# Converting the first MLP's float64 weights a feature at a time on VectorE and ScalarE, and squaring its first blocks from SBUF

## The chip, the cores and the metric

The kernel runs on one core of one Trainium2 chip. The metric is the device time of one execution in microseconds (us); the times below are medians of several executions.

## What is computed

Three stages follow one another on 3072 tokens of width 512:

```python
state = gamma * state + k[t] (outer) v[t]; y[t] = scale * q[t] @ state    # retention, 4 x 8 heads, 768 steps
x = y as (3072, 512)
r = maximum(x @ w_in, 0); x = (s * (r * r) + b) @ w_out                   # first MLP, d_ff = 2048
logits = x @ w_gate; tokens are assigned greedily to 8 experts, 384 each
out = maximum(x @ w1[e], 0) @ w2[e]                                       # second MLP, by expert
```

`w_in` and `w_out` arrive as float64. The device reads them as pairs of 32-bit words and makes two fp32r tiles of each: a high part `h` and a low part `l`. Products are formed from three matmuls (high by high, high by low, low by high).

## The kernel before, in words

The tokens are cut into 12 blocks of 256, each of two chunks of 128. The first MLP's 2048 hidden features are cut into `NF` = 16 groups, called features here; feature f has 128 rows of `w_in` (half n = 2f) and 128 of `w_out` (half n = 2f + 1), each half a tile of 128x512 numbers, or 512 KB of float64.

**Order of work.** The program writes out the order of every engine's instructions itself (`manual_schedule`). `Weave` holds a planned time `t`. Each unit of PE work (`wv.unit(cost, fn)`) adds its cost; before it is issued, every side generator whose due time has come is stepped, and each `yield` adds its number of nanoseconds to that due time. So the numbers in `CY` set how densely conversion steps lie between PE's units. They set an order, not a time: each engine then runs its own list, waiting where data or a buffer is missing.

**Prologue.** `load_chunk` (line 175) asks SP for the q, k, v and decay tiles of chunks 0 to 5, with the raw weights of halves 0 to 5 between them (lines 572 to 579, `conv_load`, line 228). The loop at line 588 alternates between `attn3`, which computes retention for blocks 0 to 2, and the weight conversion, whose steps are stretched there by `PRO` = 1.5; it stops converting early once `PN` = 2 is in `READY`. GpSimd (POOL) scales q and v (lines 201 and 204).

**Conversion** (`conv_gen`, line 233), for each half n, 512 numbers to a partition. ScalarE (ACT) squares the upper words (line 239). VectorE (DVE) shifts and masks the upper words (line 262), puts sign and exponent back (line 266), sets tiny numbers to zero by means of the squares (line 269), takes the exponent alone (line 275) and multiplies the lower word by it (line 279). ACT rounds to `h` (line 249), POOL subtracts `h` (line 251) and adds the low word (line 253) to give `l`. The raw words are read at a stride of two words, and all results go into packed tiles.

**First MLP, blocks 0 to 2** (`moe1`, line 544, called at line 597). For each feature and each of three blocks, `h_unit` (line 416) issues 12 matmuls (line 425) into one of two PSUM banks and ACT takes the Relu into `r` (line 428); `r_split` (line 433) squares it on ACT into `rh` (line 436), squares it again on DVE from the PSUM bank (line 440), and POOL forms `rl`, the low part (line 441). Two units later `x_unit` (line 450) issues 6 matmuls (line 458). That makes 48 pairs of an `h_unit` and an `x_unit`, planned at 1320 and 1300 ns. `hu` (line 552) first makes sure that the weights it needs have been converted. `r` has two buffers, `rh` and `rl` three.

**Later blocks** go one at a time, with retention and the gate's dot products (line 481) beside them. There `r_split` is called without the PSUM bank: the squares wait in `LOW`, and `low_parts` (line 444) squares `r` from SBUF (line 447) and subtracts `rh` (line 448), both on DVE, at the next `hu`. Blocks 3 to 11, the gate, the assignment and the second MLP follow.

Of the kernel before, what the change touches and what calls it, by code (L numbers as in the profile page):

```python
# [20 lines left out]
F32 = mybir.dt.float32  # L21
F32R = mybir.dt.float32r
BF = mybir.dt.bfloat16
F16 = mybir.dt.float16
I32 = mybir.dt.int32
U32 = mybir.dt.uint32
I64 = mybir.dt.int64
AF = mybir.ActivationFunctionType
OP = mybir.AluOpType
# [3 lines left out]
FAR = 1.0e6  # L33


TINY_WORD = 1.125 * 2.0 ** -15


class Side:
# [42 lines left out]
def kernel(  # L82
# [16 lines left out]
    stages=2,  # L99
    PRO=1.5,  # L100
    PN=2,
    CY=(560, 890),
    SY=(5500, 5200, 4200, 3000, 2600, 1200),
    IY=(1500, 2700, 900),
    LG=(900, 880),
# [13 lines left out]
    NF = w64.shape[0]  # L119
# [4 lines left out]
    TB = 256  # L124
# [6 lines left out]
    stage = ctx.enter_context(tc.tile_pool(name="stage", bufs=2))  # L131
# [4 lines left out]
    PE, ACT, DVE, POOL, SP = nc.tensor, nc.scalar, nc.vector, nc.gpsimd, nc.sync  # L136
# [17 lines left out]
    loads = p0.enter_context(tc.tile_pool(name="loads", bufs=2, side="right"))  # L154
# [3 lines left out]
    work = p1.enter_context(tc.tile_pool(name="work", bufs=2))  # L158
    xpool = p1.enter_context(tc.tile_pool(name="xpool", bufs=2))
    tmp = p1.enter_context(tc.tile_pool(name="tmp", bufs=6))  # L160
# [5 lines left out]
    def load_dec(j):  # L166

        if j < CPB:
            n = 2 * NF - 1 - 2 * CPB - j // 2
            QD[j] = wpool.tile([128, 512], F32, name=f"qdec{j}", tag=("h", "l")[j % 2] + str(n))  # L170
        else:
            QD[j] = loads.tile([128, 512], F32, name="qdec", tag="qdec")
        SP.dma_start(QD[j], dec[:, j % CPB * n0:(j % CPB + 1) * n0])

    def load_chunk(j):
        if j < CPB:

            ts = []
            for i in range(4):
                n = 2 * NF - 1 - 2 * j - i // 2  # L180
                tag = ("h", "l")[i % 2] + str(n)
                ts.append(wpool.tile([128, 512], F32, name=f"first{j}_{i}", tag=tag))
            for i in (0, 1, 3, 2):
                SP.dma_start(ts[i], qkv[j, :, i])
                if j == 0 and i in first:
                    first[i]()
            if j:
                load_dec(j)
        else:
            ts = []  # L190
            load_dec(j)
            for i in (0, 2):
                t = loads.tile([128, 2, 512], F32, name=f"q{i}", tag=f"q{i}")
                SP.dma_start(t, qkv[j, :, i:i + 2])
                ts += [t[:, 0, :], t[:, 1, :]]
        QKV[j] = ts

    def scale_chunk(j, q=POOL, v=POOL):
# [23 lines left out]

    W = {}
    RAW = {}
    NRAW = 6
    READY = set()

    def conv_load(n):
        pool, tag = ((stage, "sa"), (loads, "q0"), (loads, "q2"))[n // 2 % 3]
        RAW[n] = pool.tile([128, 512], I64, name="raw", tag=tag)  # L230
        SP.dma_start(RAW[n], w64[n // 2, n % 2])

    def conv_gen():
        sq = {}

        def square(n):
            hf = RAW[n].bitcast(F32).rearrange("p (n t) -> p t n", t=2)[:, 1, :]
            sq[n] = tmp.tile([128, 512], F32, name="tmp")
            ACT.activation(sq[n], hf, AF.Square)

        square(0)
        last = None

        def parts(step):
            n, a, p = last
            if step == 0:
                W[n] = (wpool.tile([128, 512], F32R, name=f"h{n}", tag=f"h{n}"),
                        wpool.tile([128, 512], F32R, name=f"l{n}", tag=f"l{n}"))
                ACT.activation(W[n][0], a, AF.Copy)
            elif step == 1:  # L250
                POOL.tensor_tensor(a, a, W[n][0].bitcast(F32), op=OP.subtract)
            else:
                POOL.tensor_tensor(W[n][1], a, p, op=OP.add)  # L253
                READY.add(n)

        for n in range(2 * NF):
            raw = RAW.pop(n)
            hi32 = raw.bitcast(I32).rearrange("p (n t) -> p t n", t=2)[:, 1, :]
            lo32 = raw.bitcast(U32).rearrange("p (n t) -> p t n", t=2)[:, 0, :]
            a = tmp.tile([128, 512], F32, name="tmp")  # L260
            ai = a.bitcast(I32)
            DVE.tensor_scalar(ai, hi32, 3, 0x3FFFFFFF, op0=OP.logical_shift_left, op1=OP.bitwise_and)  # L262
            if last:
                parts(0)
            yield CY[0]
            DVE.scalar_tensor_tensor(ai, hi32, -0x40000000, ai, op0=OP.bitwise_and, op1=OP.bitwise_or)  # L266
            yield CY[1]
            p = sq.pop(n)
            DVE.scalar_tensor_tensor(a, p, TINY_WORD * TINY_WORD, a, op0=OP.is_ge, op1=OP.mult)  # L269
            if last:  # L270
                parts(1)
            if n + 1 < 2 * NF:
                square(n + 1)
            yield CY[1]
            DVE.tensor_scalar(p.bitcast(I32), ai, -0x800000, None, op0=OP.bitwise_and)
            yield CY[0]
            if last:
                parts(2)
            DVE.scalar_tensor_tensor(p, lo32, 2.0 ** -52, p, op0=OP.mult, op1=OP.mult)
            if n + NRAW < 2 * NF:  # L280
                conv_load(n + NRAW)
            last = (n, a, p)
            yield CY[1]
        for step in range(3):
            parts(step)
            yield 600

    conv = Side(conv_gen())

# [126 lines left out]
    def h_unit(blk, f, hb):  # L416

        xh, xl = XT[blk]
        wh, wl = W[2 * f]
        ph = bank(hb)[:, 0:TB]  # L420
        n = 0
        for kc in range(KC):
            ks = slice(kc * 128, (kc + 1) * 128)
            for a, b in ((wh, xh), (wh, xl), (wl, xh)):
                PE.matmul(ph, a[:, ks], b[:, kc, :], start=(n == 0), stop=(n == 3 * KC - 1))  # L425
                n += 1
        r = work.tile([128, TB], F32, name="r", bufs=2)
        ACT.activation(r, ph, AF.Relu)  # L428
        return r, ph

    LOW = []

    def r_split(r, rh, rl, ph=None):


        ACT.activation(rh, r, AF.Square)  # L436
        if ph is None:
            LOW.append((r, rh, rl))
        else:
            DVE.scalar_tensor_tensor(r, ph, 0.0, r, op0=OP.max, op1=OP.mult)  # L440
            POOL.tensor_tensor(rl, r, rh.bitcast(F32), op=OP.subtract)
        return rh, rl

    def low_parts():
# [95 lines left out]
    def conv_until(n):  # L540
        while n not in READY:
            conv.step()

    def moe1(blks, xbs, lag, apart=0):


        units = []
        seq = [(f, i) for f in range(NF - apart) for i in range(len(blks))]
        seq += [(f, i) for i in range(len(blks)) for f in range(NF - apart, NF)]
        for n in range(len(seq) + lag):  # L550
            if n < len(seq):
                def hu(n=n):
                    f, i = seq[n]
                    conv_until(2 * f + 1)
                    low_parts()
                    r, ph = h_unit(blks[i], f, 2 + n % 2)
                    R2[blks[i], f] = r_split(r, work.tile([128, TB], F32R, name="rh", bufs=3),
                                             work.tile([128, TB], F32R, name="rl", bufs=3),
                                             ph if len(blks) > 1 else None)
                units.append((1320, hu))  # L560
            if n >= lag:
                def xu(n=n - lag):
                    f, i = seq[n]
                    if n + lag >= len(seq):
                        low_parts()
                    x_unit(blks[i], f, xbs[i])
                    if f == NF - 1:
                        x_out(blks[i])
                units.append((1300, xu))
        return units  # L570

    conv_load(0)
    load_chunk(1)
    conv_load(1)
    SP.dma_start(sb[:, 0:1], bass.AP(tensor=moe_s.tensor, offset=moe_s.offset, ap=[[0, 128], [1, 1]]))
    SP.dma_start(sb[:, 1:2], bass.AP(tensor=moe_b.tensor, offset=moe_b.offset, ap=[[0, 128], [1, 1]]))
    for j in range(2, CPB):
        load_chunk(j)
        conv_load(j)
    scale_chunk(0, DVE)  # L580

    def attn3():
# [5 lines left out]
    while not a3.done:  # L588
        if conv.due < a3.due and PN not in READY:
            t = conv.due  # L590
# [5 lines left out]
    wv = Weave([conv])  # L596
    for u in moe1((0, 1, 2), ((4, 5), (6, 7), (0, 1)), 2):
        wv.unit(*u)
    conv_until(2 * NF - 1)
    load_chunk(CPB)  # L600
    load_chunk(CPB + 1)
    scale_chunk(CPB)
# [59 lines left out]
    def h_pair(f):  # L662
        rs = []
        for i, blk in enumerate(pair):
            wv.unit(1320, lambda: rs.append(h_unit(blk, f, 2 + i)[0]))

        R4[f] = [wpool.tile([128, 512], F32R, name=f"{p}{2 * f}", tag=f"{p}{2 * f}") for p in "hl"]
        for i, r in enumerate(rs):
            r_split(r, *(t[:, i * TB:(i + 1) * TB] for t in R4[f]))
        low_parts()  # L670
# [415 lines left out]
    wv = Weave([Side(searches()), Side(indexes()), Side(weights())])  # L1086
# [91 lines left out]
```

## Time and profile before

| | us |
|---|---|
| median of 3 runs (1144.25 to 1148.87) | 1146.67 |
| the profiled execution | 1142.75 |
| its span, first to last instruction | 1141.0 |

| engine | busy us | share of the span |
|---|---|---|
| PE (TensorE matmul) | 1016.3 | 89% |
| DVE (VectorE) | 875.2 | 77% |
| ACT (ScalarE) | 385.1 | 34% |
| POOL (GpSimd) | 221.7 | 19% |

The durations used below come from the profiled execution, which is 3.9 us below the median of the runs. In a row of the trace `tmp<-raw x32` names the tile written, the tile read and the number of instructions; in a timeline the first number is the start from the beginning of the span and the second the duration. L425 is line 425. PE and PEld are TensorE's matmuls and weight loads. The first MLP's blocks 0 to 2 lie between 46.9 and 230 us of the span.

### The profile page before, as it was taken

To read this page: it belongs to the slowest core of one execution; us is meant where nothing else is said; L and a number is where in the kernel's file an instruction comes from. 1 tells how busy PE (TensorE), PEld (TensorE's weight loads), DVE (VectorE), ACT (ScalarE), POOL (GpSimd) and SP (SyncE) were. 2 spreads that over 40 slices of the span, in tenths; PEclk is the share of its full clock that TensorE was granted. 3 is DMA by queue.
4 is the path that set the end of the run, shared out by engine and by line. 5 is a ranking of instruction groups with operands and counts; after the bars stand their busy time and mean duration, and the time that the engine had idled before them with its cause. 6 is when DMAs were issued, how large, how long until landed. Compare 5 with 4: busy or idle time off the path is not lost.

```text
span 1141.0 us, 19761 instructions
## 1 busy us (share of the span) xinstructions
PE 1016.3 (89%) x7636; PEld 875.8 (77%) x7636; DVE 875.2 (77%) x2114; ACT 385.1 (34%) x802; POOL 221.7 (19%) x211
## 2 busy tenths in 40 slices
PE   5887877899999999999998999578789888888997
PEld 4766666788889898989897888467677677776786
DVE  3899999669999999999964744667787787867642
ACT  2433333332323323223333331223333443333442
POOL 3777777620000000000000000010111102011211
PEclk8999999999999999999999999869799999999999
DMA  9422222262212121221121000322333333343540
GB/s 323 144 90 92 93 93 82 96 193 75 66 47 75 56 57 56 57 74 58 35 95 32 2 1 11 138 66 85 120 102 121 111 108 134 95 133 116 166 139 28
DMA packets 35040, 104.51 MB, mean 92 GB/s; under 512 B 4737, under 2 KB 5249, under 8 KB 34945
## 3 DMA queue, kind: packets, MB, share of 16 engines
q1 hardware_dynamic: 30528, 89.60, 24.2%
q0 software_dynamic: 3840, 12.59, 3.3%
q8 instruction: 60, 0.98, 0.3%
q10 hardware_dynamic: 576, 1.05, 0.3%
q14 instruction: 36, 0.29, 0.1%
HBM read 90.64 MB, written 12.58 MB: 90 GB/s over the span
## 4 chain that ended last, share of the span: by engine, by line
PE 55%; DVE 23%; issue 11%; DMA 5%; ACT 2%; POOL 2%; SPq 0%; POOLq 0%; DVEq 0%; ACTq 0%
PE b L425 17%; PE b L458 13%; PE b L1012 6%; PE b L1033 5%; PE b L687 3%; DVE tmp L262 3%; DMA big<-x2d,idx 3%; DVE l L990 2%; PE b L794 2%; PE b L358 2%; PE b L368 2%; DVE tmp L266 2%; PE b L338 2%; DVE tmp L269 2%; DVE cmp L787 2%
## 5 line engine op out<-in xcount | busy, mean ns | idle before, releaser
L425 PE MATMUL b<-xh,h 128*128 128x256 f32 x704 | 201.7, 287 | 22.6 <-DVE r L440 20.9
L481 DVE SCALAR_TENSOR_TENSOR scr<-tmp,wg 128x512 bf16<-128x512 f32 x288 | 198.3, 689 | 6.8 <-ACT tmp L468 1.8
L425 PE MATMUL b<-xh,l 128*128 128x256 f32 x704 | 199.5, 283 | 0.9 <-POOL l L253 0.9
L425 PE MATMUL b<-xl,h 128*128 128x256 f32 x704 | 199.3, 283 | 0.0
L425 PEld LDWEIGHTS b<-xh,h 128*128 128x128 f32 x704 | 134.4, 191 | 39.2 <-DVE r L440 31.1
L428 ACT ACTIVATE r<-b 128x256 f32<-128x256 f32 x192 | 73.2, 382 | 253.3 <-PE b L425 225.5
L425 PEld LDWEIGHTS b<-xl,h 128*128 128x128 f32 x704 | 134.4, 191 | 4.8
L425 PEld LDWEIGHTS b<-xh,l 128*128 128x128 f32 x704 | 134.6, 191 | 1.5 <-POOL l L253 1.5
L458 PE MATMUL b<-h,rh 128*128 128x512 f32 x320 | 130.3, 407 | 0.0
L458 PE MATMUL b<-h,rl 128*128 128x512 f32 x320 | 127.1, 397 | 2.7 <-DVE rl L448 2.7
L458 PE MATMUL b<-l,rh 128*128 128x512 f32 x320 | 127.4, 398 | 0.0
L950 POOL DMA_INDIRECT big<-x2d,idx x24 | 26.1, 1088 | 355.1 <-issue 152.6
L1012 PE MATMUL b<-gh,h 128*128 128x384 f32 x256 | 93.1, 364 | 0.0
L1033 PE MATMUL b<-h,hh 128*128 128x512 f32 x192 | 81.0, 422 | 13.3 <-ACT hh L1015 13.3
L1012 PE MATMUL b<-gl,h 128*128 128x384 f32 x256 | 88.2, 344 | 1.7 <-DVE gl L962 1.7
L1012 PE MATMUL b<-gh,l 128*128 128x384 f32 x256 | 87.8, 343 | 0.0
L990 DVE TENSOR_TENSOR l<-eraw,h 128x512 fp32r<-128x512 f32 x128 | 82.3, 684 | 6.6 <-ACT h L989 6.6
L1033 PE MATMUL b<-h,hl 128*128 128x512 f32 x192 | 78.9, 411 | 8.0 <-DVE hl L1021 7.8
L447 DVE TENSOR_TENSOR r<-r 128x256 f32<-128x256 f32 x144 | 60.7, 421 | 25.6 <-ACT h L436 17.9
L1015 ACT ACTIVATE hh<-b 128x384 fp32r<-128x384 f32 x64 | 31.3, 489 | 138.3 <-PE b L1012 138.3
L1033 PE MATMUL b<-l,hh 128*128 128x512 f32 x192 | 76.9, 401 | 0.0
L458 PEld LDWEIGHTS b<-h,rl 128*128 128x128 f32 x320 | 61.0, 191 | 19.3 <-DVE rl L448 5.5
(193 smaller groups left out, 2054.2 us busy)
## 6 DMA issues: line engine op xcount, KB each, us to landing
eraw<-in_w_dram SPq DMA_DIRECT2D x64, 512.0 KB, 3.6
q<-in_qkv_dram SPq DMA_DIRECT2D x36, 512.0 KB, 4.7
raw<-in_w_dram SPq DMA_DIRECT2D x32, 512.0 KB, 3.5
first<-in_qkv_dram SPq DMA_DIRECT2D x24, 256.0 KB, 6.0
qdec<-in_dec_dram SPq DMA_DIRECT2D x24, 256.0 KB, 2.7
x2d<-tmp SPq DMA_DIRECT2D x20, 256.0 KB, 3.8
wg<-in_wgT_dram SPq DMA_DIRECT2D x4, 512.0 KB, 3.6
x2d<-tmp ACTq DMA_DIRECT2D x4, 256.0 KB, 2.0
```

The lines of the kernel that those rows point to most:

```text
L262: DVE.tensor_scalar(ai, hi32, 3, 0x3FFFFFFF, op0=OP.logical_shift_left, op1=OP.bitwise_and)
L425: PE.matmul(ph, a[:, ks], b[:, kc, :], start=(n == 0), stop=(n == 3 * KC - 1))
L428: ACT.activation(r, ph, AF.Relu)
L447: DVE.tensor_tensor(r, r, r, op=OP.mult)
L458: PE.matmul(X2[blk][t], a[:, ts], b, start=(f == 0 and i == 0), stop=(f == NF - 1 and i == 2))
L481: DVE.scalar_tensor_tensor(scr, x, 1.0, WG[e], op0=OP.mult, op1=OP.mult, accum_out=of[:, e:e + 1])
L687: PE.matmul(XB[c], a[:, cs], b, start=(f == 0 and i == 0), stop=(f == NF - 1 and i == 2))
L950: POOL.indirect_dma_start(out=xg[:, t, :], out_offset=None, in_=x2d[:, :], in_offset=bass.IndirectOffsetOnAxis(ap=IDX[i][:, t:t + 1], axis=0))
L990: DVE.tensor_tensor(lo, raw[:, a, :], hi.bitcast(F32), op=OP.subtract)
L1012: PE.matmul(PH[0], a[:, ks], b[:, kc, :], start=(kc == 0 and n == 0), stop=(kc == KC - 1 and n == 2))
L1015: ACT.activation(hh, PH[0], AF.Relu)
L1033: PE.matmul(Y[i, t], a[:, ts], b, start=(f == 0 and j == 0), stop=(f == NF2 - 1 and j == 2))
```

## The change

The conversion takes a whole feature at a time, 1024 numbers to a partition, and works in the raw tile itself: `hi` and `hf` are views of the upper words, `lo` and `lf` of the lower words, both at a stride of two words. ACT writes the magnitude of the upper words into a packed tile `c`. DVE takes its maximum with `ZERO_WORD`, shifts and masks it, puts sign and exponent back into the raw tile, takes the exponent alone into `c`, multiplies the lower words in the raw tile, and now also subtracts `h` and adds the low word, in halves. POOL has no part in it. The raw tile shares two buffers of 8 KB to a partition with the later chunks' q, k and v. `READY` counts features. `r_split` no longer has the form that reads the PSUM bank, so blocks 0 to 2 square from SBUF on DVE as the later ones do.

```diff
-TINY_WORD = 1.125 * 2.0 ** -15
+ZERO_WORD = 2.0 ** -15
...
-    CY=(560, 890),
+    CY=(700, 1200, 650),
...
+            t = loads.tile([128, 4, 512], F32, name="q")
             for i in (0, 2):
-                t = loads.tile([128, 2, 512], F32, name=f"q{i}", tag=f"q{i}")
-                SP.dma_start(t, qkv[j, :, i:i + 2])
-                ts += [t[:, 0, :], t[:, 1, :]]
+                SP.dma_start(t[:, i:i + 2], qkv[j, :, i:i + 2])
+                ts += [t[:, i, :], t[:, i + 1, :]]
...
-    NRAW = 6
...
-    def conv_load(n):
-        pool, tag = ((stage, "sa"), (loads, "q0"), (loads, "q2"))[n // 2 % 3]
-        RAW[n] = pool.tile([128, 512], I64, name="raw", tag=tag)
-        SP.dma_start(RAW[n], w64[n // 2, n % 2])
+    def conv_load(f):
+        RAW[f] = loads.tile([128, 1024], I64, name="raw", tag="q")
+        for i in range(2):
+            SP.dma_start(RAW[f][:, i * 512:(i + 1) * 512], w64[f, i])
...
     def conv_gen():
...
+        mag = {}
+
+        def magnitude(f):
+            mag[f] = stage.tile([128, 1024], F32, name="c", tag="sa")
+            ACT.activation(mag[f], RAW[f].bitcast(F32).rearrange("p (n t) -> p t n", t=2)[:, 1, :], AF.Abs)
+
+        magnitude(0)
+        for f in range(NF):
+            raw = RAW.pop(f)
+            (_, hi), (_, hf), (lo, _), (lf, _) = (
+                [v[:, t, :] for t in range(2)] for v in
+                (raw.bitcast(d).rearrange("p (n t) -> p t n", t=2) for d in (I32, F32, U32, F32)))
+            c = mag.pop(f)
+            ci = c.bitcast(I32)
+
+            DVE.tensor_scalar(c, c, ZERO_WORD, None, op0=OP.max)
+            yield CY[0]
+            DVE.tensor_scalar(ci, ci, 3, 0x3FFFFFFF, op0=OP.logical_shift_left, op1=OP.bitwise_and)
+            yield CY[0]
+
+            DVE.scalar_tensor_tensor(hi, hi, -0x40000000, ci, op0=OP.bitwise_and, op1=OP.bitwise_or)
+            for i in range(2):
+                n = 2 * f + i
                 W[n] = (wpool.tile([128, 512], F32R, name=f"h{n}", tag=f"h{n}"),
                         wpool.tile([128, 512], F32R, name=f"l{n}", tag=f"l{n}"))
-                ACT.activation(W[n][0], a, AF.Copy)
...
+                ACT.activation(W[n][0], hf[:, i * 512:(i + 1) * 512], AF.Copy)
+            yield CY[1]
+
+            DVE.tensor_scalar(ci, hi, -0x800000, None, op0=OP.bitwise_and)
             yield CY[0]
...
+            DVE.scalar_tensor_tensor(lf, lo, 2.0 ** -52, c, op0=OP.mult, op1=OP.mult)
             yield CY[1]
...
+            for i in range(2):
+                h, l = W[2 * f + i]
+                part = slice(i * 512, (i + 1) * 512)
+                DVE.tensor_tensor(hf[:, part], hf[:, part], h.bitcast(F32), op=OP.subtract)
+                yield CY[2]
+                DVE.tensor_tensor(l, hf[:, part], lf[:, part], op=OP.add)
+                if f + 1 < NF and not i:
+                    magnitude(f + 1)
+                yield CY[2]
+            if f + 2 < NF:
+                conv_load(f + 2)
+            READY.add(f)
...
-    def r_split(r, rh, rl, ph=None):
+    def r_split(r, rh, rl):
...
         ACT.activation(rh, r, AF.Square)
-        if ph is None:
-            LOW.append((r, rh, rl))
-        else:
-            DVE.scalar_tensor_tensor(r, ph, 0.0, r, op0=OP.max, op1=OP.mult)
-            POOL.tensor_tensor(rl, r, rh.bitcast(F32), op=OP.subtract)
+        LOW.append((r, rh, rl))
         return rh, rl
...
-                    conv_until(2 * f + 1)
+                    conv_until(f)
...
     conv_load(0)
     load_chunk(1)
-    conv_load(1)
...
     for j in range(2, CPB):
         load_chunk(j)
-        conv_load(j)
+        if j == 3:
+            conv_load(1)
...
-    conv_until(2 * NF - 1)
+    conv_until(NF - 1)
```

## Rows read from the trace of the kernel before

**Rows 1.** Windows: stretch, its us, then busy us and count of each engine, clock, DMA.
```profile
80.00:100.00 20.00, 15.04 (x89) 11.92 (x88) 19.66 (x23) 8.06 (x17) 15.08 (x13) 1.00 0.32 106
214.70:230.20 15.50, 15.50 (x93) 13.54 (x91) 2.43 (x6) 7.04 (x15) 9.60 (x11) 1.00 0.30 96
```

**Rows 2.** Waits of PE, 47 to 230 us: total, times, longest, in us.
```profile
PE b L425 <- DVE r L440: 32.1, 34, 2.1
```

**Rows 3.** Groups by line and shape, 0 to 225 us: busy us, mean ns.
```profile
L251 POOL TENSOR_TENSOR tmp<-tmp,h 128x512 f32<-128x512 f32 x32 | 51.7, 1617 | 3.0 <-ACT h L249 3.0
...
L279 DVE SCALAR_TENSOR_TENSOR tmp<-raw,tmp 128x512 f32<-128x512 uint32 x32 | 38.8, 1213 | 0.9
L269 DVE SCALAR_TENSOR_TENSOR tmp<-tmp 128x512 f32<-128x512 f32 x32 | 38.0, 1189 | 0.8
...
L262 DVE TENSOR_SCALAR tmp<-raw 128x512 int32<-128x512 int32 x32 | 36.4, 1136 | 0.0
L266 DVE SCALAR_TENSOR_TENSOR tmp<-raw,tmp 128x512 int32<-128x512 int32 x32 | 32.4, 1013 | 0.9
...
L275 DVE TENSOR_SCALAR tmp<-tmp 128x512 int32<-128x512 int32 x32 | 23.5, 735 | 0.7
...
L440 DVE SCALAR_TENSOR_TENSOR r<-b,r 128x256 f32<-128x256 f32 x47 | 19.4, 414 | 8.8 <-ACT rh L436 8.8
```

**Rows 4.** Timeline of POOL and of DVE, 42 to 45 us: start, duration.
```profile
44.99 1.52 POOL L251 TENSOR_TENSOR tmp<-tmp,h 128x512 f32<-128x512 f32 x1 [3.00 <-ACT h L249]
...
42.43 0.69 DVE L279 SCALAR_TENSOR_TENSOR tmp<-raw,tmp 128x512 f32<-128x512 uint32 x1
...
44.23 0.42 DVE L262 TENSOR_SCALAR tmp<-raw 128x512 int32<-128x512 int32 x1
44.69 0.69 DVE L266 SCALAR_TENSOR_TENSOR tmp<-raw,tmp 128x512 int32<-128x512 int32 x1
```

**Rows 5.** The page's group of L990; below it DVE's timeline, 251 to 258 us.
```profile
L990 DVE TENSOR_TENSOR l<-eraw,h 128x512 fp32r<-128x512 f32 x128 | 82.3, 684 | 6.6 <-ACT h L989 6.6
...
251.15 0.42 DVE L448 TENSOR_TENSOR rl<-r,rh 128x256 fp32r<-128x256 f32 x1
251.49 0.68 DVE L481 SCALAR_TENSOR_TENSOR scr<-tmp,wg 128x512 bf16<-128x512 f32 x1
...
256.51 0.42 DVE L447 TENSOR_TENSOR r<-r 128x256 f32<-128x256 f32 x1
...
257.38 0.69 DVE L481 SCALAR_TENSOR_TENSOR scr<-tmp,wg 128x512 bf16<-128x512 f32 x1
```

**Rows 6.** Groups of ACT by line and shape, 0 to 225 us.
```profile
L239 ACT ACTIVATE tmp<-raw 128x512 f32<-128x512 f32 x32 | 21.5, 676 | 60.6 <-POOL l L253 60.6
L249 ACT ACTIVATE h<-tmp 128x512 fp32r<-128x512 f32 x32 | 20.2, 632 | 36.0 <-DVE tmp L269 35.9
L436 ACT ACTIVATE rh<-r 128x256 fp32r<-128x256 f32 x47 | 19.6, 418 | 1.5
...
L428 ACT ACTIVATE r<-b 128x256 f32<-128x256 f32 x47 | 17.5, 372 | 10.0 <-PE b L425 9.9
```

**Rows 7.** Timeline of PE, the stage's first matmul and one pair near its end.
```profile
46.88 0.39 PE L425 MATMUL b<-xh,h 128*128 128x256 f32 x1 [1.41 <-DVE xls L377]
...
216.18 0.28 PE L425 MATMUL b<-xhs,h 128*128 128x256 f32 x1
...
217.62 0.40 PE L458 MATMUL b<-h,rh 128*128 128x512 f32 x1
...
219.00 0.28 PE L425 MATMUL b<-xh,h 128*128 128x256 f32 x1
...
229.96 0.39 PE L458 MATMUL b<-h,rl 128*128 128x512 f32 x1
```

**Rows 8.** Timeline of DVE, 214.6 us: the first square after the last conversion.
```profile
214.60 0.41 DVE L440 SCALAR_TENSOR_TENSOR r<-b,r 128x256 f32<-128x256 f32 x1
```

**Rows 9.** The window 10 to 20 us, and the page's row of raw's loads.
```profile
10.00:20.00 10.00, 4.85 (x64) 4.46 (x64) 1.88 (x3) 1.19 (x3) 3.80 (x4) 0.66 1.03 351
...
raw<-in_w_dram SPq DMA_DIRECT2D x32, 512.0 KB, 3.5
```

More of the change, by code (lines that the diff above doesn't have):

```diff
@@ L224 @@
     RAW = {}
-    NRAW = 6
     READY = set()
-    def conv_load(n):
-        pool, tag = ((stage, "sa"), (loads, "q0"), (loads, "q2"))[n // 2 % 3]
-        RAW[n] = pool.tile([128, 512], I64, name="raw", tag=tag)
-        SP.dma_start(RAW[n], w64[n // 2, n % 2])
+    def conv_load(f):
+        RAW[f] = loads.tile([128, 1024], I64, name="raw", tag="q")
+        for i in range(2):
+            SP.dma_start(RAW[f][:, i * 512:(i + 1) * 512], w64[f, i])
     def conv_gen():
[L234 to L246, printed above, removed]
+        mag = {}
[17 more added lines that the diff above has]
+                n = 2 * f + i
@@ L247, in parts @@
                 W[n] = (wpool.tile([128, 512], F32R, name=f"h{n}", tag=f"h{n}"),
                         wpool.tile([128, 512], F32R, name=f"l{n}", tag=f"l{n}"))
-                ACT.activation(W[n][0], a, AF.Copy)
-            elif step == 1:
-                POOL.tensor_tensor(a, a, W[n][0].bitcast(F32), op=OP.subtract)
-            else:
[L253 to L264, printed above, removed]
+                ACT.activation(W[n][0], hf[:, i * 512:(i + 1) * 512], AF.Copy)
@@ L265, in conv_gen @@
+            yield CY[1]
+            DVE.tensor_scalar(ci, hi, -0x800000, None, op0=OP.bitwise_and)
             yield CY[0]
-            DVE.scalar_tensor_tensor(ai, hi32, -0x40000000, ai, op0=OP.bitwise_and, op1=OP.bitwise_or)
+            DVE.scalar_tensor_tensor(lf, lo, 2.0 ** -52, c, op0=OP.mult, op1=OP.mult)
             yield CY[1]
[L268 to L286, printed above, removed]
+            for i in range(2):
[7 more added lines that the diff above has]
+                yield CY[2]
@@ L428, in h_unit @@
         ACT.activation(r, ph, AF.Relu)
-        return r, ph
+        return r
     LOW = []
-    def r_split(r, rh, rl, ph=None):
+    def r_split(r, rh, rl):
         ACT.activation(rh, r, AF.Square)
-        if ph is None:
-            LOW.append((r, rh, rl))
-        else:
-            DVE.scalar_tensor_tensor(r, ph, 0.0, r, op0=OP.max, op1=OP.mult)
-            POOL.tensor_tensor(rl, r, rh.bitcast(F32), op=OP.subtract)
+        LOW.append((r, rh, rl))
         return rh, rl
@@ L553, in hu @@
                     f, i = seq[n]
-                    conv_until(2 * f + 1)
+                    conv_until(f)
                     low_parts()
-                    r, ph = h_unit(blks[i], f, 2 + n % 2)
+                    r = h_unit(blks[i], f, 2 + n % 2)
                     R2[blks[i], f] = r_split(r, work.tile([128, TB], F32R, name="rh", bufs=3),
-                                             work.tile([128, TB], F32R, name="rl", bufs=3),
-                                             ph if len(blks) > 1 else None)
+                                             work.tile([128, TB], F32R, name="rl", bufs=3))
                 units.append((1320, hu))
@@ L664, in h_pair @@
         for i, blk in enumerate(pair):
-            wv.unit(1320, lambda: rs.append(h_unit(blk, f, 2 + i)[0]))
+            wv.unit(1320, lambda: rs.append(h_unit(blk, f, 2 + i)))
         R4[f] = [wpool.tile([128, 512], F32R, name=f"{p}{2 * f}", tag=f"{p}{2 * f}") for p in "hl"]
```

## The prediction

> **What bounds the kernel now.** I read the windows first. In the window from 80 us VectorE is busy 19.66 of 20 us, while PE is not full, and the windows around it up to 214.7 us look the same; from there on it is the other way round, PE busy throughout and VectorE 2.43 of 15.5 us [rows 1]. So the first MLP's blocks 0 to 2 have two parts: one that VectorE sets, while it converts weights, and a short one that PE sets, after the last conversion. The list of waits says the same: PE waits 32.1 us for the square on line 440, the VectorE instruction that frees its PSUM bank [rows 2].
>
> The next view is the list of groups with shapes kept apart. VectorE's five conversion instructions for a half have means of 1.136, 1.013, 1.189, 0.735 and 1.213 us, together 5.29 us [rows 3]. The reader is to see that these are not what such instructions need. While POOL sits idle (3.00 us before 44.99) the same lines take 0.42 us (line 262) and 0.69 us (lines 266 and 279) [rows 4]. With 0.42 for line 275 and 0.69 for line 269, packed forms of the same width, a half would need 2.91 us. The other 2.38 us are lost beside POOL's subtraction and addition, 1.62 us the first of them [rows 3]; over 32 halves that is 76 us. The square from PSUM does not suffer: 0.414 us in the mean.
>
> The two boundaries: the first matmul of the stage starts at 46.88 us, the last at 229.96, so that it ends about 230.3 [rows 7]. The first square behind the last conversion is at 214.60 [rows 8].
>
> **The conversion's new price.** A packed fp32 instruction with two inputs takes 0.42 us for 256 numbers (line 447) and 0.684 us for 512 (line 990), 0.264 us more for 256 more [rows 5]; 1024 then take 0.684 + 2 x 0.264 = 1.21 us. Line 262, with one input, takes 0.42 for 512 at a stride of two [rows 4], what two inputs need for 256; for 1024 I take 0.68. A feature now has three instructions with one input (3 x 0.68 = 2.04), two of 1024 with two inputs (2.42), and four halves of subtraction and addition (4 x 0.684 = 2.74): 7.20 us. Each waits for the one before. Line 262's 0.42 from 44.23 is followed at 44.69 [rows 4], a gap of 0.04; at 0.03 each, nine gaps make 0.27. A feature costs **7.47 us**, against 2 x 5.29 = 10.6 before, although VectorE has taken over POOL's part.
>
> Two prices have no row. The maximum is a form that no wide instruction here has; at one number a step it is 1.21 instead of 0.68, 0.53 us a feature more, 7.4 us in 14 features. I take 0.68, as it has one input like line 262. Writing at a stride of two is not in the rows either: between nothing and double the time per number. I take nothing, since reading at this stride costs nothing (line 266 takes 0.69, as a packed instruction does); the other end is a rival below.
>
> The fixed part of an instruction matters here, since the change makes fewer and wider ones. In the rows 256 numbers take 0.42 us from SBUF (line 447) and 0.414 from PSUM (line 440) [rows 3, 5]: squaring from SBUF gains nothing per instruction. The Trainium skill, VectorE: DVE Perf Modes, section "The TRN2 errata", has 58 cycles plus the numbers at 0.96 GHz from SBUF and 120 from PSUM: 0.59 us for 512, where the rows have 0.684, and a feature at an estimated 6.4 us. By that 14 features would take some 15 us less than I sum up; the same page says that this formula is too low for single instructions, and the trace agrees with that.
>
> **The squares.** 48 squares of 0.414 us leave; two instructions from SBUF come, at the next unit. From 256.51 to the next instruction at 257.38 such a pair takes 0.87 us; its second alone, 251.15 to 251.49, takes 0.34, which with 0.46 for the first would be 0.80 [rows 5]. I take **0.85 us**. PE's bank is now freed by ACT's Relu alone, so the 32.1 us of waits for line 440 go. What is late next is `rl`: `x_unit` waits for VectorE's subtraction instead. `r` has two buffers, so the Relu of unit n waits for the pair of n - 2; `h_unit` runs two units ahead, so this costs nothing of its own.
>
> **Order and sum.** The planned costs decide how many pairs lie between conversion steps. A feature's steps add up to 3 x 700 + 2 x 1200 + 4 x 650 = 7100 ns; in the prologue, stretched by 1.5 from 3000 on, 10650 each: features 0 and 1 fit before retention's last due time of 24000, but for a last subtraction and addition (1.4 us). That is 2 x 7.47 - 1.4 = 13.5 us of VectorE where now three halves at the mean make 15.9. So I leave the stage's start at 46.9, within 2 us. The 14 features left are 99400 planned ns, at 2620 a pair 38 pairs. VectorE:
>
> 46.9 + 1.4 + 14 x 7.47 (104.6) + 38 x 0.85 (32.3) = **185.2 us** for the last conversion (214.6 now).
>
> Per pair VectorE then needs 2620 / 7100 x 7.47 + 0.85 = 3.6 us, PE 2.82 (216.18 to 219.00 [rows 7]), so VectorE still sets the pace. Behind it PE has left the `x_unit`s of pairs 38 to 47 at 1.38 us and seven `h_unit`s at 1.44 (217.62 parts the two [rows 7]): 13.8 + 10.1 = 23.9. The stage ends at **209.1** instead of 230.3: **21.2 us** less. PE alone would need 48 x 2.82 = 135 us, so it can't end before 183.
>
> **What rides along, at nothing.** ACT: for a feature two roundings of 0.632, the magnitude of 1024 (0.676 for 512, 0.418 for 256, hence 1.19), and three times 0.372 + 0.418 make 4.8 us [rows 6] of some 10; VectorE's pace covers it. SP: a feature's two loads of 512 KB, 3.5 us each to landing [rows 9], are now issued when the feature two before has left its buffer, and have a whole feature's 7 us; without that cover, 2 to 4 us a feature. In the prologue chunk 1 stands behind one more load, 512 KB at 351 GB/s or 1.5 us [rows 9], chunks 3 and 5 behind one fewer. POOL's queue keeps only the scalings, which no longer stand behind subtractions. The chunk loads and the gate's weights behind the conversion wait for the raw tiles, free at 185, over 20 us before use. Everything after the stage moves forward unchanged.
>
> The profiled execution took 1142.75 us and would take 1121.5. The median of the runs is 3.9 us above it, so on that scale 1146.67 - 21.2 = **1125.5**.
>
> **The rivals.**
> - *Writing at a stride is dear.* 3072 numbers of a feature are written into the raw tile (two times 1024, two halves). At double time they cost 3072 / 256 x 0.264 = 3.2 us more, 44 us in 14 features and some 3 in the prologue: 1125.5 + 47 = 1172, slower than now. It decides from 1.5 us a feature on, when such a write costs half as much again. Against it: strided reads are free [rows 4]. Chance 0.08. The Trainium skill, SBUF — State Buffer, section on the DMA port swizzle, says that access is at full rate while two accesses fall into a line of 16 bytes, as they do here; no run here shows it for writes.
> - *VectorE waits for ACT.* If the write of `lf`, between the words that ACT reads as `hf`, waits for both roundings, VectorE has only 0.71 us of work to cover 2 x 0.632 and the hand-over: 0.65 us a feature; with a Relu and a square ahead on ACT up to 2. In 14 features 9 to 28 us: 1134 to 1153. For it: `h` now stands in the middle of the feature's own chain, where before it was a half behind. Against it: the pairs of squares fall into that gap too. Chance 0.13.
> - *Instructions overlap more.* An instruction that waits for nothing starts 0.08 us before its predecessor ends (251.15 plus 0.42, next at 251.49 [rows 5]). If all nine did, 1 us a feature, 14 us: 1111.5. Their data depend on each other, so 0.05. The cycle counts of the skill's VectorE page, weighed above, would end near the same time, and their chance lies in this one.
> - *POOL is not what slows VectorE.* Then the factor 5.29 / 2.91 stays: 13.6 us a feature, 86 us more, 1211. The short instructions beside an idle POOL speak against it. Chance 0.04.
>
> **How the numbers follow.** The forecast has 0.70, with 1116 to 1134 (the maximum at half speed, the start, 0.3 us in a feature). About 0.5% (5.7 us) is what a measurement can tell from no change. All of the forecast and of the overlap is faster by more; of ACT's waits 0.04 faster, 0.06 the same, 0.03 slower; the other two are slower. Faster 0.79, same 0.06, slower 0.15. The range runs from the overlap, 1110, to 1146, which leaves out the dear writes, POOL's rival and the upper third of ACT's waits: 0.16 or so.
>
> **What would show it.** In the new profile the wide instructions with two inputs should take about 1.21 us and those with one 0.68, nearly without spread; POOL should have only scalings before 230 us; PE's waits should name the subtraction on line 448's successor; the last conversion should fall near 185 us and the stage end near 209. Instructions on the raw tile well over 1.3 us, VectorE idle behind ACT's roundings, or a maximum at 1.21 would prove the steps named above wrong.

## The result and the profile after

The changed kernel takes 1131.95 us (median of 4 runs, 1129.96 to 1133.87), the kernel before in the same comparison 1145.46 us. The ratio is 0.988, with an interval from 0.985 to 0.992: **faster by 1.2%**, clear of what the runs differ by. The forecast was 1125.5 us with a range from 1110 to 1146; the gain was foretold at 21.2 us and is 13.5.

Four rows of the windows of the changed kernel (stretch, its us, then busy us and count of PE, PEld, DVE, ACT and POOL, clock, DMA share, GB/s):

```profile
30.00:40.00 10.00, 5.95 (x46) 5.30 (x48) 7.73 (x9) 2.16 (x4) 5.61 (x4) 0.50 0.23 81
...
80.00:100.00 20.00, 18.40 (x111) 15.04 (x110) 19.10 (x31) 9.72 (x20) 0.00 (x0) 1.00 0.30 105
...
200.00:214.70 14.70, 14.70 (x94) 12.89 (x94) 4.01 (x10) 6.91 (x14) 0.00 (x0) 1.00 0.24 80
214.70:230.20 15.50, 12.24 (x145) 11.15 (x142) 6.66 (x14) 3.89 (x10) 2.53 (x2) 0.89 0.55 180
```

Between 80 and 100 us VectorE is still the full engine (19.10 of 20 us), but PE now works 18.40 us there instead of 15.04 [rows 1], and POOL nothing. The first row shows what I had not foreseen: between 30 and 40 us, before the stage, PE is busy 5.95 us at a granted clock of 0.50, its lower level of 1.2 GHz; in the same stretch of the kernel before it is busy 7.98 us at a mean of 0.91.

The groups of VectorE in the stage, 57 to 180 us, against rows 3:

```profile
L270 DVE TENSOR_TENSOR l<-raw 128x512 fp32r<-128x512 f32 x26 | 18.0, 691 | 0.8
L268 DVE TENSOR_TENSOR raw<-raw,h 128x512 f32<-128x512 f32 x26 | 17.8, 685 | 0.0
L263 DVE SCALAR_TENSOR_TENSOR raw<-raw,c 128x1024 f32<-128x1024 uint32 x13 | 15.9, 1224 | 0.3
L253 DVE SCALAR_TENSOR_TENSOR raw<-raw,c 128x1024 int32<-128x1024 int32 x13 | 15.9, 1223 | 0.3
L434 DVE TENSOR_TENSOR rl<-r,rh 128x256 fp32r<-128x256 f32 x36 | 15.3, 425 | 3.5
L433 DVE TENSOR_TENSOR r<-r 128x256 f32<-128x256 f32 x36 | 15.1, 419 | 0.0
L250 DVE TENSOR_SCALAR c<-c 128x1024 int32<-128x1024 int32 x14 | 9.7, 693 | 0.4
L248 DVE TENSOR_SCALAR c<-c 128x1024 f32<-128x1024 f32 x14 | 9.6, 686 | 0.0
L261 DVE TENSOR_SCALAR c<-raw 128x1024 int32<-128x1024 int32 x13 | 9.0, 691 | 0.3
```

A feature is 0.686 + 0.693 + 1.223 + 0.691 + 1.224 + 2 x 0.685 + 2 x 0.691 = 7.27 us, where two halves cost 10.6 before. Writing into the raw tile at a stride of two costs nothing (1.22 us at lines 253 and 263, where I had 1.21 for a packed form), and the maximum on line 248 takes 0.686 us as the other instructions with one input do.

PE's timeline at the joints (start, duration, instructions, idle time before and what ended it), the last line from the kernel before, the others from the changed one:

```profile
34.05 2.35 PE L348 MATMUL b<-am,first 128*64 128x128 f32 x15 [7.36 <-DVE am L334]
...
47.20 2.35 PE L348 MATMUL b<-am,first 128*64 128x128 f32 x15 [2.62 <-DVE am L334]
...
55.47 0.39 PE L415 MATMUL b<-xh,h 128*128 128x256 f32 x1 [1.41 <-DVE xls L367]
...
214.16 2.06 PE L328 MATMUL b<-q 64*128 64x128 f32 x32
...
224.04 1.95 PE L328 MATMUL b<-q 64*128 64x128 f32 x16 [3.13 <-POOL q L201]
...
237.36 1.16 PE L338 MATMUL b<-q 64*128 64x128 f32 x16
```

The stage starts at 55.47 us, **8.6 later** than before [rows 7], and ends at 214.16, **16.1 earlier**. So the stage itself has shrunk by 24.7 us, from 183.4 to 158.7. Behind it the first matmul on chunk 8 comes 9.9 us after the stage's end, where it came 7.1 us after it before (237.36, with the stage's end at 230.28): PE waits 3.13 us for a scaled chunk. After that stretch the kernel stands 12.2 us ahead, matmul for matmul, and holds that up to about 700 us of the span; the profiled execution gives 3 of them back in the last third, in stretches that the change doesn't touch. The medians differ by 13.5.

The list of waits names what PE waits for instead of line 440 [rows 2], as foretold, the subtraction that makes `rl`:

```profile
PEld b L444 <- DVE rl L434: 28.2, 31, 2.5
...
PE b L444 <- DVE rl L434: 15.2, 29, 2.0
```

### The profile page after: what moved, and what is told of

Same layout as the page of the kernel before. It is cut to its first block, busy times and chain, and to the rows that moved or that the text cites. A ratio compares the mean times of both kernels' runs of the same rounds, so it can differ in the third digit from the quotient of the medians.

```text
span 1132.1 us, 19567 instructions
## 1 busy us (share of the span) xinstructions
PE 1017.9 (90%) x7636; PEld 878.7 (78%) x7636; DVE 849.0 (75%) x2146; ACT 382.1 (34%) x786; POOL 79.1 (7%) x99
## 4 chain that ended last, share of the span: by engine, by line
PE 57%; DVE 25%; issue 7%; DMA 5%; ACT 2%; POOL 2%; SPq 0%; POOLq 0%; DVEq 0%; ACTq 0%
PE b L415 17%; PE b L444 14%; PE b L997 7%; PE b L1018 6%; PE b L672 3%; DMA big<-x2d,idx 3%; PE b L779 2%; DVE scr L467 2%; DVE l L975 2%; PE b L348 2%; PE b L358 2%; DVE raw L253 2%; DVE r L433 2%; DVE raw L263 2%; PE b L328 2%
## 5 line engine op out<-in xcount | busy, mean ns | idle before, releaser
L415 PE MATMUL b<-xh,h 128*128 128x256 f32 x704 | 199.3, 283 | 1.4 <-DVE xls L367 1.4
L433 DVE TENSOR_TENSOR r<-r 128x256 f32<-128x256 f32 x192 | 81.6, 425 | 38.4 <-ACT rh L426 20.4
L434 DVE TENSOR_TENSOR rl<-r,rh 128x256 fp32r<-128x256 f32 x160 | 68.7, 429 | 14.5 <-PE b L415 0.5
```

The lines of the kernel that those rows point to most:

```text
L433: DVE.tensor_tensor(r, r, r, op=OP.mult)
L434: DVE.tensor_tensor(rl, r, rh.bitcast(F32), op=OP.subtract)
```

## The experiments

All times are medians of runs beside the kernel before on the same chip; the ratio is to that kernel, which took 1143.5 to 1145.5 us in these comparisons. "Start" and "end" are the first matmul of the first MLP and the end of its blocks 0 to 2 in PE's timeline. Where a run is compared with the changed kernel, it is by what each lies below or above the kernel before in its own comparison (the changed one 13.5 us below). Each kernel has one profile: with the same order of work ahead of the stage the start differs by 1.1 us (46.9 before, 45.8 in e8_sbuf), so shifts of that size say nothing.

| | us | ratio, interval | start | end | length |
|---|---|---|---|---|---|
| before | 1145.5 | 1 | 46.9 | 230.3 | 183.4 |
| after | 1132.0 | 0.988, 0.985 to 0.992 | 55.5 | 214.2 | 158.7 |
| e1_loads | 1128.7 | 0.987, 0.985 to 0.990 | 51.0 | 211.2 | 160.2 |
| e2_later | 1131.2 | 0.988, 0.986 to 0.991 | 52.4 | 212.6 | 160.2 |
| e3_split | 1123.6 | 0.982, 0.979 to 0.985 | 54.0 | 210.9 | 156.9 |
| e4_pace | 1123.7 | 0.982, 0.978 to 0.987 | 51.9 | 204.0 | 152.0 |
| e5_all | 1112.0 | 0.973, 0.970 to 0.975 | 44.6 | 193.4 | 148.8 |
| e6_gpsimd | 1169.0 | 1.022, 1.018 to 1.026 | 57.8 | 249.1 | 191.3 |
| e7_psum | 1146.8 | 1.002, 1.000 to 1.004 | 55.7 | 229.3 | 173.6 |
| e8_sbuf | 1153.0 | 1.008, 1.005 to 1.011 | 45.8 | 239.1 | 193.3 |
| e9_mid | 1113.3 | 0.974, 0.972 to 0.976 | 48.2 | 200.6 | 152.4 |
| e10_whole | 1115.7 | 0.973, 0.970 to 0.976 | 46.6 | 198.6 | 152.0 |

**The prologue.** The trace of the changed kernel shows how it comes late. VectorE's timeline, 24 to 36 us:

```profile
24.38 1.64 DVE L250 TENSOR_SCALAR c<-c 128x1024 int32<-128x1024 int32 x1
26.05 1.95 DVE L253 SCALAR_TENSOR_TENSOR raw<-raw,c 128x1024 int32<-128x1024 int32 x1
29.89 0.69 DVE L367 SCALAR_TENSOR_TENSOR xl<-b,xh 128x512 fp32r<-128x512 f32 x1 [1.89 <-ACT xh L366]
...
31.22 2.17 DVE L263 SCALAR_TENSOR_TENSOR raw<-raw,c 128x1024 f32<-128x1024 uint32 x1
33.31 2.47 DVE L334 TENSOR_TENSOR am<-b,mask 128x512 f32<-128x512 f32 x4
```

and ACT's:

```profile
28.04 1.20 ACT L258 ACTIVATE h<-raw 128x512 fp32r<-128x512 f32 x2 [4.42 <-DVE raw L253]
29.26 0.60 ACT L366 ACTIVATE xh<-b 128x512 fp32r<-128x512 f32 x1
```

Attention's copy `xh` at 29.26 stands behind two roundings, which wait 4.42 us for line 253; VectorE's `xl` waits for `xh`; and the masked scores (line 334), which PE waits 7.36 us for, stand behind all of that and behind line 263. On top of it the long instructions run into POOL's scalings of the chunks (23.93 to 26.9 and 30.92 to 36.5 us in POOL's timeline) and take 1.64, 1.95 and 2.17 us instead of 0.69 and 1.23.

Not all of the 8.6 us arises in these queues. In PE's timeline chunk 2's product with the masked scores starts 5.6 us later than before (34.05 against 28.45), and chunk 4's 7.5 us later (47.20 against 39.72). The rest comes while PE works on these two chunks behind its waits of 7.36 and 2.62 us. Its work on chunk 2 lasts 5.43 us at a granted clock of 0.50 (before, 4.20 us at a mean of 0.60), that on chunk 4 lasts 4.35 us at a mean of 0.66 (before, 3.24 us at 1.00): 2.3 us more together. No run keeps the clock apart from the waits.

*e1_loads* (`conv_load` now takes the halves that it is to load):

```diff
...
-    conv_load(0)
+    conv_load(0, (0,))
     load_chunk(1)
+    conv_load(0, (1,))
...
-        if j == 3:
-            conv_load(1)
+        if j in (2, 3):
+            conv_load(1, (j - 2,))
```

> Undoes the order of the first raw loads alone: the halves of features 0 and 1 are asked for one at a time behind chunks 0, 1, 2 and 3, as in the kernel before; all else as changed. Theory A (the prologue's 8.6 us are lost in the in-order queues of VectorE and ScalarE, where long conversion instructions stand ahead of attention's): the first matmul of the first MLP moves from 55.5 us to about 54, and the time by 0 to 2 us. Theory B (the loads: chunk 1 waits for 512 KB more, and what follows is late with it): the first matmul comes back to about 47 us and the time falls by about 8 us.

The start moves to 51.0, 4.5 us: between the two. VectorE's timeline of this run:

```profile
23.01 0.69 DVE L251 TENSOR_SCALAR c<-c 128x1024 int32<-128x1024 int32 x1
23.73 1.23 DVE L254 SCALAR_TENSOR_TENSOR raw<-raw,c 128x1024 int32<-128x1024 int32 x1
...
28.20 1.23 DVE L264 SCALAR_TENSOR_TENSOR raw<-raw,c 128x1024 f32<-128x1024 uint32 x1
29.34 2.48 DVE L335 TENSOR_TENSOR am<-b,mask 128x512 f32<-128x512 f32 x4
```

Attention is 1.3 us earlier from the start (`xh` at 19.48 instead of 20.75), and the same three instructions no longer meet a scaling: 0.69, 1.23, 1.23 us, 2.6 us less. So the place of the loads itself cost about 1.3 us; a larger part, 2.6 us, came from where it put the conversion against POOL. On the whole time this run can't be told from the changed kernel (0.987 against 0.988).

*e2_later*: the two roundings move behind the `yield` that follows line 253.

```diff
-                ACT.activation(W[n][0], hf[:, i * 512:(i + 1) * 512], AF.Copy)
             yield CY[1]
+            for i in range(2):
+                ACT.activation(W[2 * f + i][0], hf[:, i * 512:(i + 1) * 512], AF.Copy)
             DVE.tensor_scalar(ci, hi, -0x800000, None, op0=OP.bitwise_and)
```

> Issues the two roundings of a feature one conversion step later, so that in ScalarE's queue attention's copy of a chunk no longer stands behind roundings that wait for VectorE; all else as changed. Theory A: the first matmul of the first MLP comes 2 to 3 us earlier (about 53 us), the time falls by as much; in the stage itself VectorE may wait for the roundings by up to 0.7 us a feature, 0 to 8 us in all. Theory B (loads): the first matmul stays within 1 us of 55.5.

The start moves to 52.4, 3.1 us, as theory A has it. ACT's timeline shows the place changed:

```profile
24.61 0.60 ACT L367 ACTIVATE xh<-b 128x512 fp32r<-128x512 f32 x1 [0.66 <-PE b L359]
...
28.46 1.24 ACT L261 ACTIVATE h<-raw 128x512 fp32r<-128x512 f32 x2 [2.59 <-DVE raw L253]
```

The stage is 1.5 us longer and the time the same within the intervals, so this edit alone is a shift in the trace and no gain in the time, though theory A gave one.

**Chunk 8.** *e3_split*: the raw tiles get a pool that is closed at the conversion's end, and the later chunks two tiles each in its space.

```diff
...
-            t = loads.tile([128, 4, 512], F32, name="q")
             for i in (0, 2):
-                SP.dma_start(t[:, i:i + 2], qkv[j, :, i:i + 2])
+                t = QP[0].tile([128, 2, 512], F32, name=f"q{i}", tag=f"q{i}")
+                SP.dma_start(t, qkv[j, :, i:i + 2])
...
     conv_until(NF - 1)
+    pr.close()
+    QP.append(p0.enter_context(tc.tile_pool(name="qs", bufs=2, side="right")))
```

> Gives the later chunks' q, k and v two tiles each again, as before the change (in space that the raw tiles leave free when the conversion has ended); all else as changed. Theory C (the 3.9 us lost between 214 and 230 us come from the one tile that holds all four parts: chunk 8's load waits until chunk 6 has been read whole): PE's wait of 3.1 us for the scaling of chunk 8 goes, and the time falls by about 4 us. Rival (the stretch is slow since TensorE's clock fell there, or since GpSimd scales late): the time stays within 1 us.

The time falls by some 7 us (20.4 us below the kernel before), more than expected. In PE's timeline the matmuls on chunk 8 stand 7.0 us behind the stage's end (210.85), where they stood 7.1 before the change and 9.9 after it:

```profile
217.85 1.16 PE L331 MATMUL b<-q 64*128 64x128 f32 x16 [0.25 <-POOL q L204]
```

In SP's timeline chunk 8's first load starts 1.2 us after the stage's end here (212.08), and 4.2 us after it in the changed kernel (218.32): there it waits until all four parts of chunk 6 have been read. In the profile the lead over the changed kernel is 7.7 us behind that stretch, and 4.4 of them arise in it, as theory C has it, 2.9 up to chunk 8's first matmul. The other 3.3 are not chunk 8: the start is 1.5 us earlier, for which no run shows a cause, and the stage 1.8 shorter, since the later loads put POOL's scalings of chunks 6 and 7 behind the conversion. In the changed kernel those of chunk 6 (182.46 to 186.29 us in POOL's timeline) fall into feature 15, where lines 263 and 268 take 1.8 us more than alone:

```profile
183.19 2.21 DVE L263 SCALAR_TENSOR_TENSOR raw<-raw,c 128x1024 f32<-128x1024 uint32 x1
185.31 1.53 DVE L268 TENSOR_TENSOR raw<-raw,h 128x512 f32<-128x512 f32 x1
...
188.95 0.69 DVE L270 TENSOR_TENSOR l<-raw 128x512 fp32r<-128x512 f32 x1
```

**VectorE's order.** *e4_pace*:

```diff
-    CY=(700, 1200, 650),
+    CY=(800, 1400, 730),
```

> Raises the planned cost of the conversion steps from 7100 to 8320 ns a feature, so that fewer conversion steps lie between two pairs and the conversion ends nearer to the stage's end; all else as changed. Theory D (VectorE converts too early and idles at the end while PE still has ten pairs to do): the last conversion moves from 189.6 to about 196 us, the stage's end from 214.2 to about 205, and the time falls by 6 to 10 us. In the prologue the longer steps shift by some hundred ns, so the first matmul may move by 2 us either way. Rival (VectorE's total work sets the end, whatever the order): the end stays at 214 and the time within 2 us.

The time falls by some 7 us (20.3 us below the kernel before). The last conversion ends at 192.6 instead of 189.6 (196 were expected), the stage at 204.0 instead of 214.2: its length is 6.7 us less. Behind the last conversion PE needs 11.4 us instead of 24.5, so fewer pairs are left for a time in which VectorE has little to do: theory D. The other 3.5 us come from the start, more than the 2 us allowed, since the longer steps happen to put attention's masked scores ahead of conversion instructions (42.53 and 44.33 in VectorE's timeline, one chunk at a time). Of both, 10.2 us, the next stretch gives back 1.1.

**GpSimd.** *e6_gpsimd*: four instructions on a tile of its own in each feature from the third on.

```diff
...
+        def busy():
+            POOL.tensor_tensor(idle, idle, idle, op=OP.mult)
...
             DVE.tensor_scalar(ci, hi, -0x800000, None, op0=OP.bitwise_and)
+            if f > 1:
+                busy()
+                busy()
...
                 DVE.tensor_tensor(hf[:, part], hf[:, part], h.bitcast(F32), op=OP.subtract)
+                if f > 1:
+                    busy()
```

> Adds four multiplications of 128x512 numbers on GpSimd to each feature from the third on, on a tile that nothing else reads, so that VectorE's own list is the same; all else as changed. Theory P (a VectorE instruction that reads SBUF through two inputs or two ports stands still while GpSimd works): VectorE's conversion instructions spread from 0.69 and 1.23 us up to two times that, each GpSimd instruction costs VectorE about 0.7 us, 56 of them some 40 us; the last conversion moves from 189.6 to about 225 us and the time rises by about 30 us. Rival (the old spread came from the data waits of the old conversion, not from GpSimd): durations stay as they are, the time within 2 us.

They wait for nothing, so POOL runs all 56 between 35.4 and 115 us, 16 of them before the stage starts, and one run holds both cases. VectorE's groups from 57 to 115 us, with POOL busy 54.9 of 58 us:

```profile
L444 DVE TENSOR_TENSOR r<-r 128x256 f32<-128x256 f32 x8 | 10.0, 1256 | 0.0
L445 DVE TENSOR_TENSOR rl<-r,rh 128x256 fp32r<-128x256 f32 x8 | 8.8, 1101 | 0.6
L281 DVE TENSOR_TENSOR l<-raw 128x512 fp32r<-128x512 f32 x6 | 8.6, 1430 | 0.2
...
L259 DVE SCALAR_TENSOR_TENSOR raw<-raw,c 128x1024 int32<-128x1024 int32 x3 | 6.1, 2019 | 0.0
...
L254 DVE TENSOR_SCALAR c<-c 128x1024 f32<-128x1024 f32 x3 | 4.6, 1525 | 0.0
```

and from 120 to 180 us, with POOL idle:

```profile
L259 DVE SCALAR_TENSOR_TENSOR raw<-raw,c 128x1024 int32<-128x1024 int32 x7 | 8.6, 1225 | 0.2
...
L281 DVE TENSOR_TENSOR l<-raw 128x512 fp32r<-128x512 f32 x12 | 8.3, 690 | 0.4
...
L445 DVE TENSOR_TENSOR rl<-r,rh 128x256 fp32r<-128x256 f32 x17 | 7.2, 425 | 1.8
L444 DVE TENSOR_TENSOR r<-r 128x256 f32<-128x256 f32 x17 | 7.1, 419 | 0.0
...
L254 DVE TENSOR_SCALAR c<-c 128x1024 f32<-128x1024 f32 x6 | 4.1, 686 | 0.0
```

The same instructions take 0.68 to 0.84 us longer, whatever their own length (0.419 to 1.256, 0.425 to 1.101, 0.690 to 1.430, 1.225 to 2.019, 0.686 to 1.525; the four groups not shown lie between). In these 58 us VectorE runs 43 instructions and POOL 41, so about one of POOL's falls to each of VectorE's, as if each stood still for part of one GpSimd instruction. The last conversion ends at 223.1 us, near the 225 that theory P gave; the stage is 32.6 us longer than the changed kernel's, 0.8 us for each of the 40 that run in it, and the time rises by some 38 us where 30 were expected. The Trainium skill, SBUF — State Buffer, section "Who interferes with whom", says that whoever issues first holds the shared port pair for the whole instruction; a surcharge that doesn't grow with VectorE's instruction agrees with that.

**The two parts singly.** *e7_psum* undoes the squares: `r_split` takes the PSUM bank again (`DVE.scalar_tensor_tensor(r, ph, ...)`, `POOL.tensor_tensor(rl, r, rh, ...)`), the conversion stays as changed.

> Undoes the squares alone: blocks 0 to 2 square from the PSUM bank on VectorE and GpSimd forms the low part, as before; the conversion as changed. By VectorE's own work a pair costs 0.34 us instead of 0.85, 19 us less up to the last conversion. Theory P: GpSimd's 0.94 us for each low part stands in VectorE's way, 0.5 to 0.7 us a pair, which gives 19 to 27 us back, and PE waits for its bank again; the time comes to within 8 us of the changed kernel's, on either side. Rival (no contention): the time falls by 10 us or more.

It is as slow as the kernel before, some 16 us above the changed one: twice as much as theory P allowed. Its groups from 57 to 180 us:

```profile
L431 POOL TENSOR_TENSOR rl<-r,rh 128x256 fp32r<-128x256 f32 x32 | 37.4, 1168 | 102.1 <-DVE r L430 99.8 <-PE b L415 2.4
...
L268 DVE TENSOR_TENSOR raw<-raw,h 128x512 f32<-128x512 f32 x22 | 18.3, 830 | 0.0
...
L253 DVE SCALAR_TENSOR_TENSOR raw<-raw,c 128x1024 int32<-128x1024 int32 x12 | 15.9, 1328 | 0.3
...
L430 DVE SCALAR_TENSOR_TENSOR r<-b,r 128x256 f32<-128x256 f32 x33 | 13.8, 418 | 16.6 <-ACT rh L426 16.6
```

One GpSimd instruction to a pair is enough to stretch the conversion (0.685 to 0.830, 1.223 to 1.328). And the square from PSUM is issued with its own unit: VectorE waits 16.6 us for ACT's square, with the conversion's instructions queued behind it, a wait that I had left out. VectorE's timelines weigh the two. From the stage's start to the last conversion its conversion instructions sum to 119.4 us here and 104.2 in the changed kernel, its squares to 16.7 and 32.5: what the squares save, GpSimd takes back, as theory P has it. The last conversion's end, 149.4 us behind the start instead of 134.2, is later by 15.2 us, about the wait for ACT.

*e8_sbuf* is the kernel before with `r_split` called without the bank.

> The kernel before with the squares from SBUF alone: conversion on VectorE, ScalarE and GpSimd as before. VectorE's work rises by 0.5 us a pair, 21 us up to the last conversion. Theory P: GpSimd loses 48 of its instructions and VectorE gets 20 to 30 us of standing still back; the time lies within 8 us of before. Rival (no contention): some 20 us slower.

Slower by 9 us, just past theory P's 8, and by less than half of the rival's 20. VectorE has more instructions that work in SBUF alone, and they too stretch beside GpSimd; groups of VectorE from 55 to 190 us:

```profile
L447 DVE TENSOR_TENSOR r<-r 128x256 f32<-128x256 f32 x32 | 26.3, 823 | 0.0
L266 DVE SCALAR_TENSOR_TENSOR tmp<-raw,tmp 128x512 int32<-128x512 int32 x22 | 24.9, 1131 | 0.6
...
L269 DVE SCALAR_TENSOR_TENSOR tmp<-tmp 128x512 f32<-128x512 f32 x22 | 15.2, 689 | 1.3
```

Line 447 takes 0.823 us instead of 0.42 [rows 5], while line 269 has come down from 1.189 to 0.689 [rows 3]. The standing still has moved, not gone. So neither part gains anything alone (1.002 and 1.008); together, with GpSimd out of the stage but for chunk 6's scalings, they give 0.988.

**Together.** *e5_all* holds the edits of e1, e2, e3 and e4; *e9_mid* the same with CY=(760, 1310, 690); *e10_whole* those of e1, e2 and e4.

> Puts the four edits of the first runs together: raw loads by halves as before, roundings one step later, two tiles for a later chunk's parts, and the longer planned costs. If the losses are separate (prologue order, chunk 8's load, VectorE converting too early), the gains against the changed kernel add: about 3 + 2 + 5 + 9 us, and the time comes to about 1113 us, against 1144 before. Rival (all of them remove the same wait, or PE sets the stage's end once one of them is in): not under 1120 us.

> The four edits together, with planned costs between the changed kernel's and the longer ones (7660 ns a feature). With the longer ones PE waits 5.9 us for converted weights and chunk 8 waits for DMA engines that are full since every load behind the conversion starts within 20 us of the stage's end. Theory D: the conversion ends some 3 us earlier before the stage's end, which takes part of both waits away and lets VectorE idle a little longer: 1108 to 1114 us, about level with the longer costs (1112). Rival: the earlier end of the conversion is given back whole, as in the changed kernel: 1116 us or more.

> Loads by halves, roundings one step later and the longer planned costs, but one tile for all four parts of a later chunk, as in the change. Theory C: chunk 8's load waits for all of chunk 6 again, 4 us more than with the four edits together, 1116 us. Rival: with the conversion ending late, DMA is what chunk 8 waits for either way, and chunk 6's load may start when feature 14's tile is free, earlier than with separate tiles: within 2 us of 1112.

The gains add up, in the sum if not term by term: 1112 us, 32 us under the kernel before and some 19 under the changed one, with the start at 44.6, before the old 46.9. With the middle costs the time is level, as expected: the stage is 3.6 us longer, the stretch behind it 2.9 us shorter up to chunk 8's first matmul.

Whether the one tile for a chunk costs its 4 us here stays open. The medians of e5 and e10 lie 3.7 us apart, as theory C has it, but their intervals overlap almost whole, and in both traces chunk 8's first matmul comes 9.9 us after the stage's end. In e10 its load starts as late as in the changed kernel, 4.2 us after the stage's end (202.71). In e5 its first load starts 1.2 us after the stage's end (194.61), but the DMA engines are full from 185 to 200 us (busy share 1.00 to 1.02), and PE waits as long:

```profile
203.26 2.08 PE L333 MATMUL b<-q 64*128 64x128 f32 x16 [3.13 <-POOL q L204]
```

So with two tiles and a conversion that ends late another wait takes the place of theory C's; with the middle costs (e9) neither is there, and chunk 8 comes 7.0 us after the stage's end.

## Why the prediction was right, and what it missed

- **What bounds the stage**: right. The slow conversion instructions come from GpSimd; e6 shows it on an unchanged list of VectorE, and e7 and e8 show what remains when part of GpSimd's work stays. One row proves less than I read from it: line 266's 0.69 us from 44.69 [rows 4] end 0.39 us after POOL has started at 44.99, so it did not run beside an idle POOL throughout; lines 262 and 279 did.
- **The conversion's price**: 7.20 us of durations forecast, 7.27 measured (7.47 was the forecast with its gaps). The two prices without a row, the maximum and writing at a stride, came out as taken; that rival is out.
- **Order and sum**: 38 pairs lie before the last conversion, as worked out (10 squares follow it). From the stage's start to the last conversion's end it took 134.2 us instead of 138.3, and the tail 24.5 instead of 23.9. The stage is 158.7 us long, 162.2 were forecast. The mis-sized term is the gaps, 0.27 us a feature or 3.8 in 14: where an instruction follows one on other tiles it starts before that one's end (58.87 behind 58.52 plus 0.43, a conversion step behind a square in VectorE's timeline), and the durations in that stretch sum to more than the stretch, 136.7 us. That much of the rival "Instructions overlap more" was true.
- **The stage's start**: this is the step that failed, "I leave the stage's start at 46.9, within 2 us". I compared sums of VectorE's work and not their order. The prologue is a chain through several engines' queues, and a long instruction ahead of attention's delays it; the start came 8.6 us late, 2.3 of them with PE at a lower clock behind the longer waits. e1 and e2 take 4.5 and 3.1 us of it back, and together with the new order of e5 all of it. I had costed the changed load order at nothing, set nothing for conversion instructions that meet POOL's scalings in the prologue, and left out that roundings stand ahead of attention's copies in ACT's queue.
- **"Over 20 us before use"**: held for chunks 6 and 7, but not for chunk 8, which waits for chunk 6's tile; the gate's last weights are loaded at 210.04, 12 us before their use, without a wait. A tile that is released whole cost 2.9 us up to chunk 8's first matmul (e3).
- **VectorE waits for ACT**: this rival did not come in the stage (no idle time before line 268), but in the prologue VectorE waited 1.89 us for ACT's `xh`, which stood behind the two roundings.

So 21.2 became 13.5: the stage gave 3.5 us more, the start took 8.6 and the stretch behind the stage 3.9; the 1.3 left lie within what the runs differ by. That the time still came near the forecast is in part luck: two losses of 12.5 us, for which 2 us had been allowed, were eased by a stage that went faster than its sum.

## What to carry to other kernels

Where an engine's instructions take longer beside GpSimd, ask what GpSimd still does in the stage after a change: here each part alone gained nothing, since the loss moved to other instructions (e8) or to a wait (e7), and the two together gained. Before moving or widening steps, follow the order in each engine's queue past the stage that is meant to gain, and ask of every merged tile who waits for its last reader. Equal sums of work in a stretch say nothing about when its chain ends.

## What the runs showed of the hardware

Beside a GpSimd that was busy 54.9 of 58 us (e6), VectorE's instructions on SBUF alone took 0.68 to 0.84 us longer each, at 0.42 us of own length as at 1.22, so short ones suffer most: line 444 took three times as long. The square that reads the PSUM bank and one SBUF tile was not slowed: in the kernel before, 11 of its 48 ran for 0.3 us or more beside a GpSimd instruction, and none took over 0.425 us (0.414 in the mean [rows 3]). e7 says nothing on this, since GpSimd waits there until the square is done (99.8 us of waits for line 430).
